# Sixteen weight requests on ScalarE's queue, a later check of alpha, and an early ScalarE copy in a gated-recurrence and SoLU kernel

## The chip, the cores and the metric

The kernel runs on one core of a Trainium2 chip. The metric is device microseconds of one execution. A run of the kernel before has seven such times; one more execution was taken by the hardware profiler, and all durations below are from that one.

## The reference

The computation is a gated linear recurrence over 768 tokens for 4 batches and 8 heads of width 48, and behind it a feed-forward block with a SoLU activation and a layer norm. Shapes and types that matter: q, k, v and alpha are float32 of (4, 8, 768, 48); w_in is (384, 1024) and w_out (1024, 384), both float64.

```python
for t in range(S):
    state = alpha[:, :, t, :, None] * state + np.einsum('bhd,bhe->bhde', k[:, :, t], v[:, :, t])
    y[:, :, t] = np.einsum('bhd,bhde->bhe', q[:, :, t], state)
...
h = x @ w_in                      # x is y as (tokens, 384)
h_max = np.max(h, axis=-1, keepdims=True)
e = np.exp(h - h_max)
sm = e / (np.sum(e, axis=-1, keepdims=True) + 1e-09)
solu = h * sm
mu = np.mean(solu, axis=-1, keepdims=True)
var = np.mean((solu - mu) ** 2, axis=-1, keepdims=True)
ln = (solu - mu) / np.sqrt(var + 1e-06) * g_ln
return (ln @ w_out).astype(np.float32)
```

## The kernel before

**Tiles and stages.** The 768 tokens are cut into six groups (g) of 128 tokens, each for all four batches. A group goes through the recurrence in matrix form (products of alpha by scans, masked scores, read-out y), and then through the feed-forward block: eight up-projections (f = 0 to 7, 512 token columns each) and the down-projections. Each head's 48 columns are split into 32 and 16; four heads' 32 rows fill the 128 partitions of one chunk, and the eight 16-row rests fill a third chunk.

**Order.** The order on every engine is written out by hand (a manual schedule): each engine takes its instructions in the order of the program text, and so does each DMA queue, SyncE's and ScalarE's. A DMA request is an instruction of the engine whose queue it goes on. A ScalarE request therefore takes ScalarE's time in its place in that order, and a wait of the request is a wait of all that stands behind it on ScalarE. Semaphores are placed by the framework; each request signals its landing on one of eight semaphores, which the requests of both queues take in turn.

**The start, group 0.** SyncE loads alpha (into `an`), k (`kn`), q (`qn`) and v, in this order; ScalarE requests four small constants (ident, mask, parity, g_rows). GpSimd clears buffers and later copies v into place (L180). TensorE runs `warm` (L422) and then turns alpha, k and q by matmuls with the identity (`turned`, L162). Ahead of each turning, ScalarE copies the last 16 columns of every head together (`ends_of`, L153), and the last third of the turning reads that copy. ScalarE copies turned alpha into `aT` (L655). VectorE scans it backwards (`scan_back`), multiplies k (L663), scans forward (`scan_on`, three parts) and multiplies q (L671): the last third first, giving `qe`, which ScalarE spreads by `apart` (L237). `alpha_over` (L201) is two ScalarE activations over the whole of `an`, whose accumulated sums a check at the end of the kernel reads. Then come the scores (L268), the mask products on VectorE (`masked`, L279), the read-out into four PSUM banks y (L300), ScalarE's four copies of y into `x` (L331), and `keys_back` (TensorE L287, ScalarE L289), whose transposes use three of the banks that y held.

**Weights.** w_in and w_out arrive as float64 words in six slots of a buffer, `room`. VectorE turns them into float32 with five instructions for a block of 768 columns (`bits`, L572 to L584); ScalarE tests their range with two activations, each with a read of its sum (`in_range`, L559 and L560). `fetch(i, slot, n)` requests block i; with n = 2 a double block (i and i + 1). For w_in a double block takes 16 requests: eight of 32 rows and eight of 16 rows, of 4 KB each row. `fetch(0, 3, 2)` and `fetch(2, 1, 2)` request all of w_in, 32 requests on SyncE behind v. `bits(0)` and `bits(1)` make the columns for f = 0 to 3 out of the first double block.

**The up stage of group 0** (the loop over f behind `in_range(1)`). `up_mm` is three matmuls (L366, which the profile shows as six), then `up_act`: Exp on ScalarE (L380), a product on VectorE (L381), Square on ScalarE (L382). PSUM has two banks for h, so that f + 2 waits for the product of f. In f = 0 follows `next_state` (TensorE L342, ScalarE L349), and the requests for w_out and the k, q and alpha of group 1.

```python
    masked(0)
    masked(1)
    bits(0)
    read_values(0)
    gains()
    keys_back(0)
    in_range(0)
    bits(1)
    in_range(1)
```

Of the kernel before, what the change touches and what calls it, by code (L numbers as in the profile page):

```python
# [11 lines left out]
U32 = mybir.dt.uint32  # L12
# [20 lines left out]
def fast_path(ctx, tc, q, k, v, alpha, moe_w_in, moe_w_out, moe_g_ln, out):  # L33
# [12 lines left out]
    nc = tc.nc  # L46
    B, H, S, D = q.shape
# [32 lines left out]
    ones = const.tile([P, P], FP, name="ones")  # L80
# [8 lines left out]
    mean_sb = const.tile([P, DM], FP, name="mean_sb")  # L89
# [10 lines left out]
    an = const.tile([P, H, TQ, D], FP, name="an")  # L100
# [36 lines left out]
    def by_token(x):  # L137

        return x.rearrange("p h u d -> p (h u d)").rearrange("p (b h d) -> p b h d", b=B, h=H)

    def load_first(src, dst, g):
        t = slice(g * P, (g + 1) * P)
        for b in range(0, B, 2):
            nc.sync.dma_start(
                out=by_token(dst)[:, b : b + 2].rearrange("p b h d -> p (b h) d"),
                in_=src[b : b + 2, :, t].rearrange("b h p d -> p (b h) d"),
            )

    def ends_of(src, tag=None):

        ends = ring.tile([P, T4], FP, name=tag) if tag else two.tile([P, T4], FP, tag="two", name="ends")
        ends = ends.rearrange("p (b d) -> p b d", b=B)
        nc.scalar.copy(out=ends.rearrange("p b (h d) -> p b h d", h=H), in_=by_token(src)[:, :, :, E0:D])  # L153
        return ends

    def turned(src, ends, out, blocks=range(NB)):

        x = by_token(src)
        for j in blocks:
            for b in range(B):  # L160
                cols = x[:, b, j, 0:E0] if j < H else ends[:, b, E0 * (j - H) : E0 * (j - H) + E0]
                nc.tensor.matmul(  # L162
                    out[j // NP][32 * b : 32 * b + 32, j % NP], lhsT=cols, rhs=ident, start=True, stop=True,
                    tile_position=(0, 32 * b), skip_group_check=True,
                )
# [9 lines left out]
    def load_v_first(slot):  # L175
        x = slots[slot].rearrange("p (n d) -> p n d", d=D)
        y = vn.rearrange("p b h d -> p (b h) d")
        nc.sync.dma_start(out=x, in_=v[:, :, 0:P].rearrange("b h p d -> p (b h) d"))
        for dst, src in ((slice(0, E0), slice(0, E0)), (slice(48, 64), slice(E0, D))):
            nc.gpsimd.tensor_copy(out=y[:, :, dst], in_=x[:, :, src])  # L180
# [16 lines left out]
    def alpha_over(g):  # L197
        x = an.rearrange("p h u d -> p (h u d)")
        sq = one.tile([P, 768], FP, name="sq").bitcast(U8)[:, 0 : x.shape[1]]
        for i, sign in enumerate((1.0, -1.0)):  # L200
            nc.scalar.activation(  # L201
                out=sq, in_=x, func=AF.Relu, scale=sign, bias=mone, accum_out=over[:, g, i : i + 1]
            )
# [12 lines left out]
    def scan_on(g, i):  # L216
        part = slice(NP * i, NP * i + NP)
        s = seed[i % 2]
        if i == 2:
            nc.vector.tensor_copy(out=fend[:, g], in_=h4[:, :, 1])  # L220

        least = small.tile([P, NP, 1], FP, name="least")
        nc.vector.tensor_scalar(out=least, in0=h4[:, part, 1:2], scalar1=LEAST, scalar2=None, op0=ALU.max)  # L223
        nc.vector.reciprocal(out=s[:, :, 0:1], in_=least)
        scan(aT[:, part], aT[:, part], s, False)
# [9 lines left out]
    def apart():  # L235
        for i in range(2):
            nc.scalar.mul(  # L237
                out=qv[:, H : 2 * H].rearrange("p (j i) t -> p j i t", i=2)[:, :, i], in_=qe, mul=parity[:, i : i + 1]
            )
# [16 lines left out]
    def quarter(b):  # L256
        return slice(32 * b, 32 * b + 32)

    def banks(name, shape, n=B):
        return [ps_a.tile([P] + shape, FP, tag=f"a{b}", name=f"{name}{b}") for b in range(n)]  # L260

    def scores(g, half, a=None):
        a = a or banks("a", [NP, P])
        for i in range(NP):
            h = half * NP + i
            for kb, qb in ((h, h), (H + h // 2, H + h)):
                for b in range(B):
                    nc.tensor.matmul(  # L268
                        a[b][:, i], lhsT=kT[quarter(b), kb], rhs=qv[quarter(b), qb], start=kb == h, stop=kb != h,
                        tile_position=(32 * b, 0), skip_group_check=True,  # L270
                    )
        masks[half] = a
# [21 lines left out]
    parts = [(a, [(NP * a + r, slice(0, E0)) for r in range(NP)]) for a in range(2)]  # L294
# [231 lines left out]

    raws = {}

    def fetch(i, slot, n=1):

        kind, f = pieces[i]
        w = n * F // (2 if kind else KC)
        raw = room[:, 1536 * slot : 1536 * (slot + n)].bitcast(U32).rearrange("p (c f w) -> p c f w", f=w, w=2)
        if kind:
            parts = [(slice(0, P), c, moe_w_out[(f + c) * P : (f + c + 1) * P, :]) for c in range(2)]
        else:
            rows = moe_w_in[:, f * P : f * P + w].rearrange("(h d) f -> h d f", d=D)
            parts = [(slice(E0 * r, E0 * r + E0), c, rows[NP * c + r, 0:E0]) for c in range(2) for r in range(NP)]
            parts += [(slice(E1 * h, E1 * h + E1), 2, rows[h, E0:D]) for h in range(H)]
        for rows, c, src in parts:  # L540
            if float64:
                nc.sync.dma_start(out=raw[rows, c].rearrange("p f w -> p (f w)"), in_=src.bitcast(U32))
            else:
                dst = w_out[rows, f + c, 0:DM] if kind else w_in[rows, c, f * P : f * P + w]
                nc.sync.dma_start(out=dst, in_=src)
        for m in range(n):
            raws[i + m] = raw[:, :, w // n * m : w // n * (m + 1)]

# [70 lines left out]
    def inline(x, name):  # L619
        return nc.inline_tensor(np.ascontiguousarray(x, np.float32), name=name).ap()  # L620

    load_first(alpha, an, 0)
    nc.scalar.dma_start(out=ident, in_=inline(np.eye(P), "ident_c"))
    nc.scalar.dma_start(out=mask, in_=inline(np.triu(np.ones((P, P))), "mask_c"))
    odd = np.arange(P) // E1 % 2
    nc.scalar.dma_start(out=parity, in_=inline(np.stack([1 - odd, odd], 1), "parity_c"))
# [9 lines left out]
        nc.gpsimd.memset(s, 0.0)  # L636
    nc.gpsimd.memset(state, 0.0)
    load_v_first(0)
    fetch(0, 3, 2)
    fetch(2, 1, 2)  # L640
    nc.vector.memset(ones, 1.0)
    nc.vector.memset(small_ones, 1.0 / 32)
    nc.vector.memset(mhalf, -0.5)
    nc.vector.memset(mone, -1.0)
# [2 lines left out]
    def three(name, where):  # L647
        return [pool.tile([P, NP, P], FP, tag=tag, name=f"{name}{i}") for i, (pool, tag) in enumerate(where)]
# [1 line left out]

    warm(18)
    t = three("tp_a", [(ps_a, "a0"), (ps_a, "a1"), (ps_a, "a2")])
    turned(an, ends_of(an), t)
    for i in range(3):
        nc.scalar.copy(out=aT[:, NP * i : NP * i + NP, 1:SW], in_=t[i])  # L655
        scan_back(0, i)
    t = three("tp_k", [(ps_a, "a3"), (ps_h, "h"), (ps_h, "h")])
    turned(kn, ends_of(kn), t)
    alpha_over(0)
    scan_on(0, 2)  # L660
    for i in range(3):
        part = slice(NP * i, NP * i + NP)
        nc.vector.tensor_tensor(out=kT[:, part], in0=t[i], in1=hk[:, part], op=ALU.mult)  # L663
    scan_on(0, 0)
    t = three("tp_q", [(ps_o, "o"), (ps_o, "o"), (ps_a, "a0")])
    turned(qn, ends_of(qn), t)
    for i in (2, 0, 1):
        if i == 1:
            scan_on(0, i)
        part = slice(NP * i, NP * i + NP)  # L670
        nc.vector.tensor_tensor(  # L671
            out=qe if i == 2 else qv[:, part], in0=t[i], in1=aT[:, part, 1:SW], op=ALU.mult
        )
        if i == 2:
            apart()
    scores(0, 0)
    t = [x.tile([P, NP, P], FP, tag=n, name="a_" + n) for x, n in ((ps_h, "h"), (ps_o, "o")) for _ in range(2)]
    scores(0, 1, t)
# [11 lines left out]
    for f in range(FC):  # L690
        p = 2 + f // 2
# [162 lines left out]
    for g in range(1, G + 1):  # L854
# [10 lines left out]
        for s in range(FC):  # L865
# [14 lines left out]
            if todo:  # L880
                n, half = todo.pop(0)
# [18 lines left out]
    parts = [N * 3, G * 2, G * NB] + [len(pieces)] * 2  # L900
    ends = np.cumsum([0] + parts)
# [4 lines left out]
    def compare(out, x, bound, op):  # L906
# [6 lines left out]
        out=chunks[:, :, 2], in0=sums[:, :, 2], scalar=0.25, in1=sums[:, :, 3], op0=ALU.mult, op1=ALU.is_le  # L913
# [6 lines left out]
    else:  # L920
# [9 lines left out]
        out=bad, in0=all_ok[0:1, 0:1], scalar1=float(P * ends[-1]), scalar2=None, op0=ALU.is_lt  # L930
# [415 lines left out]
def kernel(tc, *args):  # L1346

    with ExitStack() as ctx:
        taken = fast_path(ctx, tc, *args)
    with tc.If(taken > 0):  # L1350
        general_path(tc, *args)
# [30 lines left out]
```

## Time and profile before

| | |
|---|---|
| median of 7 runs | 399.08 us (396.38 to 401.43) |
| the profiled execution | 401.91 us |
| its span in the profile | 400.1 us |
| TensorE busy | 377.9 us, 94% |
| VectorE busy | 254.6 us, 64% |
| ScalarE busy | 146.2 us, 37% |
| GpSimd busy | 115.7 us, 29% |
| mean granted TensorE clock | 0.984 |

Times in the profile are counted from the start of the span. Engines are PE (TensorE's matmuls), PEld (its weight loads), DVE (VectorE), ACT (ScalarE), POOL (GpSimd) and SP (SyncE); an engine's name with a q is its sequencer, which issues DMA requests. L with a number is a line of the kernel before. The time of a DMA request is that of its issue; its landing comes later. Requests and waits of a sequencer are not counted as busy time.

### The profile page before, as it was taken

To read this page: it belongs to the slowest core of one execution; us is meant where nothing else is said; L and a number is where in the kernel's file an instruction comes from. 1 tells how busy PE (TensorE), PEld (TensorE's weight loads), DVE (VectorE), ACT (ScalarE), POOL (GpSimd) and SP (SyncE) were. 2 spreads that over 40 slices of the span, in tenths; PEclk is the share of its full clock that TensorE was granted. 3 is DMA by queue.
4 is the path that set the end of the run, shared out by engine and by line. 5 is a ranking of instruction groups with operands and counts; after the bars stand their busy time and mean duration, and the time that the engine had idled before them with its cause. 6 is when DMAs were issued, how large, how long until landed. Compare 5 with 4: busy or idle time off the path is not lost. (4 is left out here: it accounts for less than half of the span.)

```text
span 400.1 us, 11123 instructions
## 1 busy us (share of the span) xinstructions
PE 377.9 (94%) x4929; PEld 229.1 (57%) x4929; DVE 254.6 (64%) x415; ACT 146.2 (37%) x253; POOL 115.7 (29%) x118
## 2 busy tenths in 40 slices
PE   8786999977989999999999999999999999999995
PEld 8672435545674467556557555666556575555552
DVE  0968788997797868694574884664865413444510
ACT  2634575545314525225153243343152132223100
POOL 5010000022031893428130456210475110333200
PEclk9996999998999999999999999999999999999998
DMA  9966969601366302914040921004300000000011
GB/s 187 184 163 162 235 195 177 141 0 43 98 162 99 80 3 62 153 47 99 2 102 24 157 77 44 2 23 72 29 20 21 23 3 21 20 20 14 28 41 48
DMA packets 86409, 30.82 MB, mean 77 GB/s; under 512 B 67912, under 2 KB 84560, under 8 KB 86352
## 3 DMA queue, kind: packets, MB, share of 16 engines
q1 hardware_dynamic: 85328, 29.11, 33.9%
q8 instruction: 40, 0.66, 0.8%
q10 hardware_dynamic: 1024, 0.92, 0.7%
q14 instruction: 17, 0.14, 0.1%
HBM read 25.30 MB, written 4.72 MB: 75 GB/s over the span
## 5 line engine op out<-in xcount | busy, mean ns | idle before, releaser
L366 PE MATMUL h<-x,w_in 128*128 128x512 f32 x288 | 135.2, 610 | 4.4 <-DVE g_col L596 4.4
L477 PE MATMUL o<-w_out,room 128*128 128x385 f32 x384 | 133.2, 491 | 1.1 <-DVE least L223 1.1
L477 PEld LDWEIGHTS o<-w_out,room 128*128 128x128 f32 x384 | 71.4, 189 | 57.1 <-issue 15.5
L366 PEld LDWEIGHTS h<-x,w_in 128*128 128x128 f32 x288 | 53.3, 192 | 64.2 <-issue 51.2
L381 DVE TENSOR_TENSOR room<-h,e 128x512 f32<-128x512 f32 x40 | 27.8, 694 | 61.6 <-ACT e L380 61.6
L508 POOL TENSOR_TENSOR r<-sums,mhalf 128x1 f32<-128x1 f32 x20 | 12.2, 608 | 170.1 <-DVE sums L500 170.1
L380 ACT ACTIVATE e<-h 128x512 f32<-128x512 f32 x40 | 23.9, 596 | 91.7 <-PE h L366 91.7
L397 POOL TENSOR_TENSOR p<-p,e 128x512 f32<-128x512 f32 x30 | 41.0, 1367 | 24.7 <-ACT e L380 24.4
L382 ACT ACTIVATE u<-room 128x512 f32<-128x512 f32 x40 | 25.2, 631 | 42.4 <-DVE room L381 42.4
L279 DVE TENSOR_TENSOR sT<-a,mask 128x512 f32<-128x512 f32 x44 | 27.3, 682 | 16.0 <-PE a L268 16.0
L268 PE MATMUL a<-qv,kT 32*128 32x128 f32 x704 | 26.6, 291 | 4.9 <-DVE qv L758 2.0
L268 PEld LDWEIGHTS a<-qv,kT 32*128 32x128 f32 x704 | 23.6, 198 | 12.1 <-DVE qv L758 2.9
L397 DVE TENSOR_TENSOR p<-p,u 128x512 f32<-128x512 f32 x30 | 25.0, 833 | 8.6 <-ACT u L382 8.6
L209 DVE TENSOR_TENSOR_SCAN hT<-aT,unit 128x516 f32<-128x516 f32 x18 | 22.3, 1287 | 8.3 <-ACT aT L655 8.2
L209 DVE TENSOR_TENSOR_SCAN aT<-aT,seed 128x516 f32<-128x516 f32 x18 | 25.7, 1428 | 0.6
L300 PE MATMUL y<-sT,vn 128*32 128x128 f32 x768 | 22.8, 274 | 1.4 <-issue 0.8
L300 PEld LDWEIGHTS y<-sT,vn 128*32 128x32 f32 x768 | 20.7, 110 | 4.1 <-issue 2.6
L233 POOL TENSOR_TENSOR kT<-kT,hT 128x1024 f32<-128x1024 f32 (+1 forms) x8 | 13.3, 1686 | 30.9 <-DVE kT L184 30.9
L331 ACT COPY x<-y 128x384 f32<-128x384 f32 x24 | 11.2, 481 | 26.5 <-PE y L300 26.5
L300 PEld LDWEIGHTS y<-qv,state 32*32 32x32 f32 x1280 | 15.3, 103 | 7.6 <-issue 4.1
L300 PE MATMUL y<-qv,state 32*32 32x128 f32 x1280 | 19.0, 278 | 0.0
L201 ACT ACTIVATE sq<-an,mone 128x1536 uint8<-128x1536 f32 x12 | 18.8, 1571 | 0.2
(140 smaller groups left out, 372.5 us busy)
## 6 DMA issues: line engine op xcount, KB each, us to landing
an<-in_alpha_dram SPq DMA_DIRECT2D x20, 192.0 KB, 4.1
out_dram<-o_sb SPq DMA_DIRECT2D x20, 192.0 KB, 1.9
room<-in_moe_w_out_dram SPq DMA_DIRECT2D x8, 384.0 KB, 3.9
kn<-in_k_dram SPq DMA_DIRECT2D x16, 192.0 KB, 3.8
qn<-in_q_dram SPq DMA_DIRECT2D x16, 192.0 KB, 3.5
vn<-in_v_dram SPq DMA_DIRECT2D x5, 512.0 KB, 5.7
room<-in_moe_w_in_dram SPq DMA_DIRECT2D x16, 128.0 KB, 3.6
kn<-in_k_dram SPq DMA_DIRECT2D x4, 384.0 KB, 5.7
```

The costliest lines, as they stand in the source:

```text
L201: nc.scalar.activation(out=sq, in_=x, func=AF.Relu, scale=sign, bias=mone, accum_out=over[:, g, i : i + 1])
L209: nc.vector.tensor_tensor_scan(out=o, data0=a, data1=s, initial=1.0, op0=ALU.mult, op1=ALU.add)
L233: nc.gpsimd.tensor_tensor(out=kT[:, part], in0=kT[:, part], in1=hk[:, part], op=ALU.mult)
L268: nc.tensor.matmul(a[b][:, i], lhsT=kT[quarter(b), kb], rhs=qv[quarter(b), qb], start=kb == h, stop=kb != h, tile_position=(32 * b, 0), sk ...
L279: nc.vector.tensor_tensor(out=sT[:, b, half * NP : half * NP + NP], in0=a[b], in1=mask[:, None, :].to_broadcast([P, NP, P]), op=ALU.mult,)
L300: nc.tensor.matmul(y_bank(b)[quarter(r), a], lhsT=lhsT, rhs=rhs, start=(b, r) not in begun, stop=stop, tile_position=(row, 32 * r), skip_g ...
L366: nc.tensor.matmul(h, lhsT=w_in[:, a, f * P : (f + 1) * P], rhs=d["x"][:, a].rearrange("p b t -> p (b t)"), start=(a == 0), stop=(a == KC ...
L380: nc.scalar.activation(out=e, in_=h, func=AF.Exp)
L381: nc.vector.tensor_tensor(out=u, in0=h, in1=e, op=ALU.mult)
L382: nc.scalar.activation(out=u2, in_=u, func=AF.Square)
L397: eng.tensor_tensor(out=p, in0=d[0][i] if f == 1 else p, in1=d[f][i], op=ALU.add)
L477: nc.tensor.matmul(d["o"][:, 0 : DM + 1], lhsT=u_of(g, f)[:, b * P : b * P + P], rhs=w_out[:, f], start=(f == 0), stop=(f == FC - 1), skip ...
```

## The change

`fetch` takes a queue and a slice of its requests. The first two double blocks of w_in are requested in two halves: the eight 32-row requests of each stay on SyncE's queue in their old place, and the eight 16-row requests of each go on ScalarE's queue. There, five of the first block stand ahead of the `ends_of` copy of q (the copy is now issued inside the call of `turned` as before), three behind it, and the eight of the second block behind `apart`. `alpha_over(0)` moves from behind the turning of k to behind these requests. For the turning of alpha the copy of the ends is written as a statement of its own. A ScalarE copy of one column, from `ones` into `mean_sb`, which is written anew before it is read, is put between the requests for ident and mask, and the memset of `ones` is moved ahead of it.

```diff
-    def fetch(i, slot, n=1):
+    def fetch(i, slot, n=1, queue=nc.sync, some=slice(None)):
...
-        for rows, c, src in parts:
+        for rows, c, src in parts[some]:
             if float64:
-                nc.sync.dma_start(out=raw[rows, c].rearrange("p f w -> p (f w)"), in_=src.bitcast(U32))
+                queue.dma_start(out=raw[rows, c].rearrange("p f w -> p (f w)"), in_=src.bitcast(U32))
...
     load_first(alpha, an, 0)
     nc.scalar.dma_start(out=ident, in_=inline(np.eye(P), "ident_c"))
+    nc.vector.memset(ones, 1.0)
+    nc.scalar.copy(out=mean_sb[:, 0:1], in_=ones[:, 0:1])
     nc.scalar.dma_start(out=mask, in_=inline(np.triu(np.ones((P, P))), "mask_c"))
...
     load_v_first(0)
-    fetch(0, 3, 2)
-    fetch(2, 1, 2)
-    nc.vector.memset(ones, 1.0)
+    fetch(0, 3, 2, some=slice(0, H))
+    fetch(2, 1, 2, some=slice(0, H))
...
-    turned(an, ends_of(an), t)
+    ends = ends_of(an)
+    turned(an, ends, t)
...
     turned(kn, ends_of(kn), t)
-    alpha_over(0)
     scan_on(0, 2)
...
     t = three("tp_q", [(ps_o, "o"), (ps_o, "o"), (ps_a, "a0")])
+    fetch(0, 3, 2, nc.scalar, slice(H, H + 5))
     turned(qn, ends_of(qn), t)
+    fetch(0, 3, 2, nc.scalar, slice(H + 5, 2 * H))
...
         if i == 2:
             apart()
+    fetch(2, 1, 2, nc.scalar, slice(H, 2 * H))
+    alpha_over(0)
     scores(0, 0)
```

More of the change, by code (lines that the diff above doesn't have):

```diff
@@ L539, in fetch @@
             parts += [(slice(E1 * h, E1 * h + E1), 2, rows[h, E0:D]) for h in range(H)]
-        for rows, c, src in parts:
+        for rows, c, src in parts[some]:
             if float64:
-                nc.sync.dma_start(out=raw[rows, c].rearrange("p f w -> p (f w)"), in_=src.bitcast(U32))
+                queue.dma_start(out=raw[rows, c].rearrange("p f w -> p (f w)"), in_=src.bitcast(U32))
             else:
                 dst = w_out[rows, f + c, 0:DM] if kind else w_in[rows, c, f * P : f * P + w]
-                nc.sync.dma_start(out=dst, in_=src)
+                queue.dma_start(out=dst, in_=src)
         for m in range(n):
```

## The prediction

> **What bounds the kernel now.** I began with the page's slices and its chain of waits. The chain is of no use: it ends in the last output copies at 0%. The slices (10 us each) show where TensorE falters.
>
> ```profile
> PE   8786999977989999999999999999999999999995
>
> ```
>
> TensorE is busy 377.9 of 400.1 us, nearly gapless from slice 10 on; slice 3 (30 to 40 us) has both its thinnest work and its lowest clock. So time gained before 40 us can last to the end, and time lost there too. Next, the waits of the first 60 us (waiter, releaser: us in total, times, longest):
>
> ```profile
> PE h L366 <- DVE g_col L596: 4.4, 1, 4.4
> DVE top L572 <- DMA room<-in_moe_w_in_dram: 3.0, 1, 3.0
> ACT x L331 <- PE y L300: 6.7, 4, 5.6
> ```
>
> The first up-projection waits for VectorE's conversion of w_in (bits), and that waited for the transfer of the first double block. Its place, in the timeline (start, length, engine, line; in brackets the idle time before and its releaser):
>
> ```profile
> 13.08 21.60 SPq L542 DMA_DIRECT2D room<-in_moe_w_in_dram  x32
> 11.08 1.58 ACT L201 ACTIVATE sq<-an,mone 128x1536 uint8<-128x1536 f32 x1
> 14.73 0.62 ACT L153 COPY ends<-qn 128x512 f32<-128x512 f32 x1 [0.28 <-DMA qn<-in_q_dram]
> 18.54 1.33 ACT L237 ACTIVATE qv<-qe,parity 128x512 f32<-128x512 f32 x2 [3.20 <-DVE qe L671]
> 25.43 0.48 ACT L331 COPY x<-y 128x384 f32<-128x384 f32 x1 [5.55 <-PE y L300]
> 24.96 1.28 DVE L279 TENSOR_TENSOR sT<-a_o,mask 128x512 f32<-128x512 f32 x2
> 29.28 0.95 DVE L572 TENSOR_SCALAR top<-room 128x768 uint32<-128x768 uint32 x1 [3.04 <-DMA room<-in_moe_w_in_dram]
> 33.96 5.43 PE L366 MATMUL h<-x,w_in 128*128 128x512 f32 x6 [4.36 <-DVE g_col L596]
> ```
>
> SyncE issues 32 requests one by one; the sixteenth, which completes the first double block, is issued at 25.56 and lands at 29.10 (from the trace's semaphore events). VectorE was free at 26.24. ScalarE has holes of 3.2 us and 5.6 us in the same stretch. Last, the stretches by window (busy us of PE, PEld, DVE, ACT, POOL, then clock, DMA share, GB/s):
>
> ```profile
> 23.00:29.00 6.00, 5.43 (x161) 4.82 (x155) 3.24 (x6) 2.16 (x5) 0.00 (x0) 1.00 0.43 111
> 29.60:33.96 4.36, 0.00 (x1) 0.04 (x1) 4.22 (x7) 4.26 (x9) 0.00 (x0) 0.82 0.87 225
> 33.96:39.30 5.34, 5.34 (x6) 1.81 (x6) 4.21 (x5) 0.23 (x2) 0.00 (x0) 0.51 0.37 91
> ```
>
> From 23 to 29 us the DMA engines are busy 43%: issue, not bandwidth, holds the block back. And after the idle 4.36 us the clock is at half: the six matmuls take 5.43 us, against 0.43 us apiece (2.6) from 41.22 on.
>
> **What the Trainium skill says.** "DMA: Bandwidth & Descriptors", section "Issuing engines are not separate DMA queues", says that a second issuing engine saves only the sequencer's time; the 43% agrees that this is what is short here. The same page, "Anatomy of one DMA", says that a wait for a semaphore happens on the issuing sequencer before dispatch. The trace agrees: requests take eight semaphores in turn, shared by both queues (the ident request on ScalarE and the first q request on SyncE use one), and the sixteenth w_in request started at 25.56, just after the one eight before it had landed at 25.38. "TensorE: Matmul & The Clock Gate", section "Part 1: The HAM clock gate", says that an idle window of about 3.4 us halves the clock until a busy one; the trace has 0.5 from 32.41 to 39.23, two such windows.
>
> **The change, part by part** (times on the clock of the profile before).
>
> *Early copy.* The table load, 1.28 us at 6.77 behind alpha's landing, moves to about 1.0, beside the warm-up matmuls. The first aT copy then waits for tp_a alone (its 16 pairs are done near 8.05): the scans start near 8.8, not 9.27, 0.5 us less on VectorE. The requests for mask, parity and g_rows, behind the load, go out some 1.5 us later; their readers come at 18.5 or after: nothing. The memset of ones was VectorE's first anyway: nothing.
>
> *SyncE.* Sixteen of 32 requests leave its queue; pitch there is 0.46 us (0.42 and a gap). The first block keeps eight, the last issued at 20.67 before. I allow 22.6, as each waits for the semaphore of one eight before it in the mixed order, and 25.5 for the landing.
>
> *ScalarE, requests.* Sixteen issues. ScalarE's four at the start took 0.39 to 0.67, so 0.46 each, 7.4 us in all. Five sit ahead of the ends copy of qn: 11.0 to 13.3, in the hole that alpha_over leaves, before q has landed (14.65): hidden. Their 320 KB fall beside q's tail; I give that 0.4 us on q, so tp_q ends near 17.9 and VectorE's 0.5 us gain is used up: VectorE is free near 26.5. Without cover five issues would cost 2.3 us on q's path. Three issues after that copy fit before apart (18.54). Eight follow apart, from 20.3 (19.87 plus the shift). With two queues alternating over eight semaphores each queue has four in flight; 64 KB requests landed 3.1 us after issue (median). So four go at once (b1 not before v, landed 20.28 before, say 21.2), and the other four go as the first land: 23.4 to 25.8. Bounds: 24.0 without such waits, 29 if each waits for a late landing; I take 25.8.
>
> *alpha_over.* It goes from a free place at 11.08 to 14.46 into a full one: two times 1.57 and 0.19 is 3.5 us, 25.8 to 29.3. Behind it on ScalarE stand the four x copies (4 x 0.48): 29.3 to 31.2, not 25.43 to 28.53. Its reader, the check near the end, is far.
>
> *Who waits.* VectorE: bits(0) from 26.5, 4.52 us, ends 31.1, not 33.80; bits(1) at 35.6, not 38.39. TensorE: keys_back needs the banks that the x copies free, so it ends near 31.3; up_mm(0,0) starts at 31.4, not 33.96. Its window now holds the transposes and the matmuls, so it runs at full clock, 2.6 us: done at 34.0, not 39.3. ScalarE now bounds: kg copies to 32.8, in_range(0) and (1) 4.0 us to 36.8 (34.19 before), Exp 36.85, not 39.43. From here the order of before: product (VectorE) 37.5 to 38.2, Square to 38.9, two state copies (1.06) to 39.9, Exp of f=1 to 40.5 (TensorE had h at 38.6), product to 41.3, Square to 42.0, in_range(2) 1.9 to 43.9, Exp of f=2 to 44.5, product to 45.2. That product frees the bank for f=4: TensorE starts it at 45.25, not 49.23.
>
> The sum: the up stage is ahead by 4.0 us at f=4. The second half of w_in (at most 32 us) and the k, q and w_out loads that start from conversions 2 to 3 us earlier stay ahead of their readers. Nothing later has a fixed time, so the 4.0 lasts: 400.1 to 396.1 in the span. The profiled execution took 401.91 us, 1.8 around the span; the median shown is 2.8 below that, 399.08. I take 4.0 off it: **395.1**.
>
> **Rivals.**
>
> *No stall on ScalarE* (each request at 0.46): alpha_over ends at 27.5, in_range at 34.9, VectorE's bits(1) at 35.6 decides, f=4 starts near 43.7: 5.5 us, 393.6. For it: latency is 2.3 us for some requests. Against: at most four in flight.
>
> *Given back on ScalarE.* The last requests go at 29 instead of 25.8, waiting for landings on the other queue; everything behind slips by 3.2, leaving 0.8: 398.3. In this group also: TensorE idle long enough to halve the clock again, or DMA contention that delays v's landing and with it y. For it: v's and q's last share landed 1 to 1.7 us after the rest, so landings straggle. Against: DMA share 0.43 leaves room.
>
> *Slower: the five requests hold the ends copy of qn.* SyncE's own first w_in request took 4.76 us (13.08 to 17.84) behind v's. If ScalarE's five likewise wait, [...] for landings of w_in requests (the first landed at 20.87), the fifth goes out at 23, the ends copy slips from 14.73 to 23, tp_q and the qe product by 7.6, and apart, the eight requests, alpha_over and x behind: Exp near 44.5, f=4 near 52.9, 3.7 us late: 402.8. It decides from an ends copy later than about 21.5: up to there the slack of ScalarE and the regained clock pay. For it: program text puts those five after sixteen SyncE requests, and only the time order of issue, which I read from the semaphores of the first eight requests (an's second half numbered after g_rows), keeps them clear of it. Against: that same order, and ScalarE's issues at 1.6 to 2.8 us, 0.45 and 0.67 long beside a SyncE issue of 1.44.
>
> *The change does nothing* would need w_in not to be the release; the 3.0 us wait excludes it.
>
> **How the numbers follow.** Main case 0.42 (own range 392.5 to 397), no stall 0.14, given back 0.19 (397 to 401), slower 0.25. A difference under 0.5% (2 us) can hardly be told from none here. So faster is 0.42 + 0.14 + 0.02, same 0.17, slower 0.25. The range takes in all but the worst of the slow case and the quickest: 391.5 to 402.
>
> **What would show it.** Right: bits(0) starts within 1 us of VectorE's last mask product; the clock stays at 1.0 through 32 to 39; ScalarE has no wait in front of the ends copy of qn; x copies start at 28 to 30; f=4 near 45. Wrong: the ends copy of qn after 18, a hole on ScalarE of over 6 us among its requests, or x copies after 32.

## The result

The kernel after takes 403.08 us (median of 26 runs, 401.05 to 404.24), the kernel before, in runs beside it, 398.68 us (63 runs, 396.38 to 402.91). The ratio is 1.010, 95% interval 1.008 to 1.012: slower by 1%. The prediction was 395.1, with 402 as its upper end and a chance of 0.25 for slower.

The profiled execution of after took 402.0 us with a span of 400.1 us, the same span as that of before. One plain fact is needed to read that: the times of the kernel before lie in groups, 26 of the 63 at 396.4 to 397.8 us, 14 near 399 and 23 at 400.4 to 402.9, and its profiled execution (401.91) was one of the upper group. After has only one group. So the two profiles agree in span where the medians differ by 4.4 us; what parts the upper group from the rest is TensorE's clock, shown in the experiments below.

The slices of after, 10 us each: TensorE's busy share and its granted clock; the last row is the granted clock of before.

```profile
PE   8685999977979999999999999999999999999995
...
PEclk9996999999999999999999999999999999999998
...
PEclk9996999998999999999999999999999999999998
```

The dip in slice 3 (30 to 40 us) is not filled; the clock there is again 0.6. Next, what the engines waited for in after's first 60 us (waiter, releaser: us in total, times, longest).

```profile
ACT sq L201 <- DMA room<-in_moe_w_in_dram: 9.2, 1, 9.2
...
PE tp L287 <- ACT x L331: 4.8, 1, 4.8
```

VectorE's wait for the first double block shrank from 3.0 to 1.7 us, but only because VectorE came later (free at 27.66 us, 26.24 in before). In its place stand a 9.2 us hole of ScalarE ahead of `alpha_over`, among its own requests, and a 4.8 us hole of TensorE that waits for ScalarE's x copies. The places, in after's timeline (start, length, engine, line; idle time before in brackets):

```profile
16.41 0.62 ACT L153 COPY ends<-qn 128x512 f32<-128x512 f32 x1 [5.29 <-DMA qn<-in_q_dram]
...
22.71 7.78 ACTq L542 DMA_DIRECT2D room<-in_moe_w_in_dram  x8
30.54 1.58 ACT L201 ACTIVATE sq<-an,mone 128x1536 uint8<-128x1536 f32 x1 [9.24 <-DMA room<-in_moe_w_in_dram]
...
33.81 1.60 ACT L331 COPY x<-y 128x384 f32<-128x384 f32 x4
...
29.40 0.95 DVE L572 TENSOR_SCALAR top<-room 128x768 uint32<-128x768 uint32 x1 [1.74 <-DMA room<-in_moe_w_in_dram]
...
34.33 2.82 PE L287 MATMUL tp<-ident,kT 128*128 128x128 f32 x12 [4.77 <-ACT x L331]
36.94 3.82 PE L366 MATMUL h<-x,w_in 128*128 128x512 f32 x6
```

The eight requests of the second block take 7.8 us from first to last, `alpha_over` follows, then the x copies at 33.81 (25.43 in before), and with them everything of TensorE. `bits(0)` starts at 29.40, against 29.28: the first double block is not a moment earlier. The windows of after (us; busy us of PE, PEld, DVE, ACT, POOL with their instructions; clock, DMA share, GB/s):

```profile
23.00:29.00 6.00, 5.43 (x184) 5.04 (x188) 4.66 (x8) 0.00 (x0) 0.62 (x3) 1.00 0.78 202
29.60:36.94 7.34, 2.61 (x12) 2.62 (x13) 7.03 (x10) 6.02 (x10) 0.00 (x0) 0.68 0.71 144
```

From 23 to 29 us ScalarE computes nothing at all, while the DMA engines are busy 78% instead of 43%: the first block's 32-row requests, which before had gone ahead of its 16-row ones, come last now, and the second block's stand between them. From 29.6 to 36.94 TensorE works 2.6 of 7.3 us, and its clock falls again, at 32.3 us.

**Why the requests waited.** From the semaphore events of after's trace, with the landing of the request that had the same semaphore before:

```
request (issue start)                 the semaphore came free
SyncE, block 1, third        21.93    21.91  v landed
SyncE, block 1, fourth       22.29    17.10  early ScalarE request landed; queued behind the third
ScalarE, block 2, first      22.71    22.69  block 1, SyncE's first
ScalarE, block 2, second     23.07    23.00  block 1, SyncE's second
ScalarE, block 2, third      24.55    24.53  block 1, SyncE's third
ScalarE, block 2, fourth     26.78    26.76  block 1, SyncE's fourth
ScalarE, block 2, last       30.18    30.15  block 2, ScalarE's fourth
```

Eight semaphores serve both queues, so at most eight requests are in flight, whichever engine issues them, and each waits for the one eight places earlier in one common order. A request takes the semaphore whose turn it is, not one that is free: SyncE's third stood from 19.08 to 21.93 us for v's, while two of the eight, those of the early ScalarE requests, had been free since 17.10 and 17.41. A request took 2.2 to 5.7 us to land here. The 26 requests of after that were issued from 16.43 to 32.51 us came 0.64 us apart (16.08 / 25); in before, the 31 from 17.88 to 34.26 came 0.55 us apart (16.38 / 30). Two queues issued no faster than one. The early requests also changed the order: in before, the request that reuses v's semaphore is the first block's eighth, issued at 20.67 with v landed at 20.28, so that it didn't wait; in after it is SyncE's third, and it stood until v landed at 21.91.

The section "Issuing engines are not separate DMA queues" of the Trainium skill's "DMA: Bandwidth & Descriptors" says that a second issuing engine saves only the sequencer's time to start a transfer. Here it saved not even that.

### The profile page after: what moved, and what is told of

Same layout as the page of the kernel before. It is cut to its first block, busy times and chain, and to the rows that moved or that the text cites. A ratio compares the mean times of both kernels' runs of the same rounds, so it can differ in the third digit from the quotient of the medians.

```text
span 400.1 us, 11120 instructions
## 1 busy us (share of the span) xinstructions
PE 375.6 (94%) x4929; PEld 228.3 (57%) x4929; DVE 254.5 (64%) x415; ACT 146.3 (37%) x254; POOL 115.5 (29%) x118
## 3 DMA queue, kind: packets, MB, share of 16 engines
q1 hardware_dynamic: 84816, 28.06, 33.9%
## 5 line engine op out<-in xcount | busy, mean ns | idle before, releaser
L366 PE MATMUL h<-x,w_in 128*128 128x512 f32 x288 | 133.4, 603 | 0.0
L268 PE MATMUL a<-qv,kT 32*128 32x128 f32 x704 | 25.0, 278 | 4.5 <-DVE qv L763 2.0
L268 PEld LDWEIGHTS a<-qv,kT 32*128 32x128 f32 x704 | 22.0, 186 | 11.7 <-DVE qv L763 2.9
L300 PEld LDWEIGHTS y<-sT,vn 128*32 128x32 f32 x768 | 20.7, 110 | 4.4 <-issue 2.9
```

What stands on the lines that cost most here:

```text
L268: nc.tensor.matmul(a[b][:, i], lhsT=kT[quarter(b), kb], rhs=qv[quarter(b), qb], start=kb == h, stop=kb != h, tile_position=(32 * b, 0), sk ...
L300: nc.tensor.matmul(y_bank(b)[quarter(r), a], lhsT=lhsT, rhs=rhs, start=(b, r) not in begun, stop=stop, tile_position=(row, 32 * r), skip_g ...
L366: nc.tensor.matmul(h, lhsT=w_in[:, a, f * P : (f + 1) * P], rhs=d["x"][:, a].rearrange("p b t -> p (b t)"), start=(a == 0), stop=(a == KC ...
```

## The experiments

The letters in the expectations: A, the second block's requests (and what stands behind them) hold ScalarE; B, the early ScalarE requests make q late; C, the check of alpha in its new place is all the loss; D, eight requests in flight are the limit, whichever queue they are on. Key points of every profiled execution, in us of its span; "halved" is where the clock record shows 0.5 before 100 us:

| kernel | time, median | bits(0) | first x copy | f = 0 | f = 4 | halved |
|---|---|---|---|---|---|---|
| before (profile 401.91) | 398.68 | 29.28 | 25.43 | 33.96 | 49.23 | 32.4-39.2, 93.8-97.3 |
| before, a second profile (396.74) | | 27.93 | 27.08 | 32.60 | 45.26 | 20.0-23.5 |
| after | 403.08 | 29.40 | 33.81 | 36.94 | 50.61 | 32.3-39.1 |
| second block back on SyncE | 398.61 | 28.49 | 26.85 | 33.16 | 45.92 | none |
| alpha check back | 400.58 | 31.01 | 32.95 | 35.66 | 48.43 | 22.7-26.1, 94.4-97.8 |
| alpha check alone | 399.73 | 29.24 | 25.48 | 33.91 | 49.46 | 33.0-39.9, 94.5-97.9 |
| early copy alone | 399.15 | 28.83 | 25.87 | 33.50 | 47.85 | 33.9-37.3 |
| before, bridged | 397.75 | 28.34 | 25.42 | 33.01 | 45.66 | 90.9-94.4 |
| after, bridged | 403.41 | 30.55 | 34.14 | 36.02 | 49.05 | 93.9-97.3 |
| four and four | 401.35 | 29.52 | 25.26 | 34.19 | 49.45 | 32.6-39.4, 94.0-97.5 |
| v behind sixteen | 402.16 | 26.40 | 31.32 | 37.11 | 49.85 | 28.0-34.8 |
| v behind sixteen, bridged | 403.58 | 26.40 | 32.31 | 38.82 | 51.42 | 28.6-35.4, 96.9-100.3 |
| v behind four | 399.01 | 28.37 | 25.45 | 33.04 | 47.25 | 32.8-36.2 |
| v behind eight | 397.64 | 27.88 | 27.15 | 32.54 | 45.19 | 20.7-24.2 |

Where a ratio is given below, it is to the kernel before in runs beside it.

### The second block's requests back on SyncE

After, with one part undone:

```diff
-    fetch(2, 1, 2, some=slice(0, H))
+    fetch(2, 1, 2)
...
-    fetch(2, 1, 2, nc.scalar, slice(H, 2 * H))
     alpha_over(0)
```

> The eight 16-row requests of the second double block go back on SyncE's queue; all else as in the changed kernel. Theory A (ScalarE is held by those eight requests, which wait for landings between 22.7 and 30.5 us, with alpha_over and the x copies behind): ScalarE is free after apart (21.3), alpha_over ends by 25, the x copies follow TensorE's y (first near 26.9), the first up-projection starts near 32 at full clock and f=1 near 38.5, against 42.60 in the changed kernel and 41.22 before: 4 us less than the changed kernel, 2 to 3 us less than before. Theory B (the five early requests make q and v late, and with them VectorE): the gain stays away, f=1 starts at 41 or later and the time is that of the changed kernel within 1.5 us.

Measured: 398.61 us (22 runs, 397.60 to 400.97), ratio 0.998 (0.9955 to 1.0008). That is 4.5 us below after, 1% of it, and all of the loss. Its timeline:

```profile
21.20 1.56 ACT L201 ACTIVATE sq<-an,mone 128x1536 uint8<-128x1536 f32 x1
...
26.85 0.48 ACT L331 COPY x<-y 128x384 f32<-128x384 f32 x1 [2.28 <-PE y L300]
...
33.16 2.81 PE L366 MATMUL h<-x,w_in 128*128 128x512 f32 x6 [2.15 <-DVE g_col L596]
```

`alpha_over` now runs at once behind `apart`, in a hole, and ends 2.3 us before the first x copy is wanted. The x copies wait for TensorE, not for ScalarE. f = 0 starts 3.8 us earlier than in after, and its clock is whole (2.81 us against 3.82). At f = 4 the lead is 4.7 us, close to the 4.5 of the medians. So the eight requests of the second block, with the check of alpha queued behind them, are the loss, as theory A has it. The 2 to 3 us under before that were expected too did not come: with the eight requests away, the rest of the change gains nothing that can be told from zero. VectorE was free at 27.66, 1.4 us later than in before, and the first block landed at 28.31. Even with its clock whole this execution is at f = 4 no earlier than before's second profile (45.92 against 45.26).

### The check of alpha in its old place, the requests as in after

This kernel has also no early copy.

```diff
-    nc.vector.memset(ones, 1.0)
-    nc.scalar.copy(out=mean_sb[:, 0:1], in_=ones[:, 0:1])
...
     turned(kn, ends_of(kn), t)
+    alpha_over(0)
     scan_on(0, 2)
...
     fetch(2, 1, 2, nc.scalar, slice(H, 2 * H))
-    alpha_over(0)
     scores(0, 0)
```

> Requests as in the changed kernel, alpha_over back behind the turning of k, no early copy. Theory A: the eight requests still end near 30, but the x copies start there and not at 33.8: the up stage starts 3 us earlier than in the changed kernel; f=1 near 39.5, bounded by the conversion of the first block (29.4 plus 4.5): 3 us less than the changed kernel. Theory C (alpha_over's 3.5 us in the full place is all the loss): the same number, with the requests costing nothing: the wait in front of the x copies would be gone. Theory B: 1 us or less is gained, since q and v stay late.

Measured: 400.58 us (22 runs, 399.67 to 402.11), ratio 1.0045 (1.0018 to 1.0071): 2.5 us better than after, still slower than before. Its timeline:

```profile
17.88 4.13 ACTq L542 DMA_DIRECT2D room<-in_moe_w_in_dram  x3
22.06 1.33 ACT L237 ACTIVATE qv<-qe,parity 128x512 f32<-128x512 f32 x2 [4.42 <-DVE aT L209]
24.74 8.17 ACTq L542 DMA_DIRECT2D room<-in_moe_w_in_dram  x8
32.95 1.25 ACT L331 COPY x<-y 128x384 f32<-128x384 f32 x3 [9.56 <-PE y L300]
```

The first line shows the fear of the slower rival, in a milder form: behind `alpha_over` the requests come later, the ends copy of q starts at 17.02 (14.73 in before) behind the fifth of them, the three behind that copy no longer find a free semaphore (the second and third go at 21.22 and 21.62, just after landings at 21.20 and 21.60), and `apart` stands until 22.06 (18.54 in before). The releasers named in the brackets (`aT`, y) had long been done when ScalarE went on; what held it was the requests ahead in its own order. The eight then take 8.2 us and the x copies start at 32.95, not near 30 as expected, so that 2.5 of the expected 3 us came back. The wait in front of the x copies that C would have gone is still there. So the requests alone make the kernel slower, and with the check behind them (and the early copy) it is 2.2 us more at f = 4 (48.43 against 50.61).

### The two small parts, each alone

To the kernel before, the check of alpha moved behind `apart`:

```diff
-    alpha_over(0)
     scan_on(0, 2)
...
             apart()
+    alpha_over(0)
     scores(0, 0)
```

> The kernel before, with alpha_over alone moved behind apart. ScalarE is idle there for 5.55 us (19.87 to 25.43), so 3.5 us fit: theories A and B expect the time of before within 0.3% and the first x copy near 25.4. Theory C expects it late, by 3 us in the x copies, and a slower kernel only if the first block's conversion (33.8) is not later anyway: still the time of before.

Measured: 399.73 us (22 runs), ratio 1.0004 (0.997 to 1.004). The first x copy starts at 25.48 (25.43 in before), and not 3 us later as C has it. The place behind `apart` is as free as the old one, as long as no requests stand in it.

And the early copy alone:

```diff
     nc.scalar.dma_start(out=ident, in_=inline(np.eye(P), "ident_c"))
+    nc.vector.memset(ones, 1.0)
+    nc.scalar.copy(out=mean_sb[:, 0:1], in_=ones[:, 0:1])
     nc.scalar.dma_start(out=mask, in_=inline(np.triu(np.ones((P, P))), "mask_c"))
...
-    nc.vector.memset(ones, 1.0)
```

> The kernel before with the early ScalarE copy alone. The table load is hidden and the scans start 0.3 us earlier (8.96 in the changed kernel, 9.27 before); VectorE then waits for the first block of w_in as before. All theories expect the time of before within 0.3%.

Measured: 399.15 us (12 runs), ratio 1.001 (0.997 to 1.006): nothing. In its profile the scans didn't even start earlier (9.72, 8.96 expected): the turning of alpha started only at 7.88 there, behind `warm` (7.18 in before). And what the copy may give VectorE is hidden by the wait for the first block.

### Only the first block's requests on ScalarE, none ahead of q

The first block's eight 16-row requests go on ScalarE, four behind the ends copy of q and four behind `apart`; the second block is whole on SyncE and the check of alpha in its old place (the early copy stays). Against after:

```diff
-    fetch(2, 1, 2, some=slice(0, H))
+    fetch(2, 1, 2)
...
     turned(kn, ends_of(kn), t)
+    alpha_over(0)
...
-    fetch(0, 3, 2, nc.scalar, slice(H, H + 5))
     turned(qn, ends_of(qn), t)
-    fetch(0, 3, 2, nc.scalar, slice(H + 5, 2 * H))
+    fetch(0, 3, 2, nc.scalar, slice(H, H + 4))
...
-    fetch(2, 1, 2, nc.scalar, slice(H, 2 * H))
-    alpha_over(0)
+    fetch(0, 3, 2, nc.scalar, slice(H + 4, 2 * H))
```

> Only the first double block's eight 16-row requests go on ScalarE, four behind the copy of q's ends and four behind apart; the second block is all on SyncE, alpha_over back behind the turning of k, early copy kept. No request stands ahead of q's ends copy, and q has landed before they go. If early requests made q late (theory B), q lands by 14.8 and VectorE is free by 26.3; if the eight shared semaphores set the pace (theory D: eight in flight, each 3 to 4.5 us until it lands, whichever queue issues), the first block still lands no earlier than 27 us and the time is near that of the kernel with the second block back on SyncE, 398.6 us; if SyncE's issue time set it, the block lands by 25.5 and the time is 396.5 or less.

Measured: 401.35 us (22 runs, 396.51 to 402.77), ratio 1.003 (0.999 to 1.006). The time is a miss; what was expected of q and of the block came. Its timeline:

```profile
14.73 0.62 ACT L153 COPY ends<-qn 128x512 f32<-128x512 f32 x1 [0.19 <-DMA qn<-in_q_dram]
14.75 1.75 ACTq L542 DMA_DIRECT2D room<-in_moe_w_in_dram  x4
...
21.64 2.09 ACTq L542 DMA_DIRECT2D room<-in_moe_w_in_dram  x4
25.26 0.48 ACT L331 COPY x<-y 128x384 f32<-128x384 f32 x1 [5.55 <-DMA room<-in_moe_w_in_dram]
...
29.52 0.95 DVE L572 TENSOR_SCALAR top<-room 128x768 uint32<-128x768 uint32 x1 [3.44 <-DMA room<-in_moe_w_in_dram]
...
34.19 5.41 PE L366 MATMUL h<-x,w_in 128*128 128x512 f32 x6 [4.76 <-DVE g_col L596]
```

With no requests ahead of q, q landed at 14.65, as in before, against 16.33 in after and in the kernel with the second block back: B is right about q, though q is not the loss. VectorE was free at 26.07. Each queue had eight of the block's requests, ScalarE lost nothing that counted, and the block still landed at 29.34 (29.10 in before). From 18.43 to 21.64 us nothing was issued on either queue: all eight semaphores were taken, v's among them, and the next two requests went 0.02 us after landings (21.64 after 21.62, 21.81 after v's 21.79). That is what D expects: a second queue brings the block no earlier. The last lines tell where the time went: VectorE then waited 3.4 us, TensorE 4.8 us, and the clock was at half for f = 0, in this execution and probably in 14 of the 22: so many lie above 400 us, with a mean granted clock of 0.984 to 0.989 (five lie below 397.5, where before's lower group is). The number of semaphores itself wasn't varied, so D rests on the matched times of issue and landing and on this run.

### TensorE's clock: the kernel before once more, and both kernels bridged

The kernel before itself was profiled again, to see what parts its groups.

> The kernel before itself, profiled once more. Its times lie in two groups, near 397 and near 401.5. If the half-clock stretch at 93.8 us is what parts them, a run near 397 has no such stretch and is otherwise the same to within 0.3 us until 90 us; if the start parts them, f=1 does not start at 41.2.

It took 396.74 us, an execution of the lower group. Its row of the granted clock:

```profile
PEclk9989999999999999999999999999999999999998
```

The half clock lies at 20.0 to 23.5 us, on the scores, and not in the first up-projection. The scores in this profile, then in the first one:

```profile
19.61 3.46 PE L268 MATMUL a<-qv,kT 32*128 32x128 f32 x64 [2.08 <-DVE least L223]
...
19.25 2.08 PE L268 MATMUL a<-qv,kT 32*128 32x128 f32 x64 [1.74 <-DVE least L223]
```

The slow scores put off what follows: the first x copy starts at 27.08 instead of 25.43, and VectorE is free at 27.88 instead of 26.24. But the first block landed at 27.75 there, so hardly any of this delay counts. In the first up-projection a half clock counts in full: f = 0 took 2.8 us and f = 1 started at 37.24 here, against 5.4 us and 41.22 in the first profile. At f = 4 this execution is 4.0 us ahead, at the end of its span 5.2. Of that, 1.4 us stand before f = 0 and are not clock (the block landed at 27.75 and not at 29.10), 2.6 arise from f = 0 to f = 4, and the rest behind, where the first profile has a second half clock.

The mean granted clock of every execution says the same. In the 163 times of the kernel before that were taken beside the experiments, all 61 above 400 us have 0.984 to 0.989, and all 71 up to 397.8 have 0.992 to 0.998. The middle group has 0.990 to 0.996, so what parts it from the lower one stays open. Open too is what decides where the half clock falls: TensorE stood idle for 4.36 us ahead of f = 0 in the first profile and for 1.35 in the second, and the request behind v's load was held for 4.8 us in one and 3.3 in the other.

Then matmuls were added whose result isn't used, to keep TensorE busy: eight in the kernel before, behind `keys_back(0)`, where it waits for `bits(0)`; sixteen in after, ahead of `keys_back(0)`, where it waits for the x copies. (The profile shows each of them as two.)

```diff
     keys_back(0)
+    warm(8)
     in_range(0)
```

> The kernel before, with eight extra 128x128 matmuls (some 1.7 us) on TensorE between keys_back(0) and the first up-projection; their result is not used. If the two groups of its times (near 397 and near 401) come from the halved TensorE clock in the first up-projection, the clock stays at 1.0 from 30 to 40 us, the group near 401 disappears and the median falls to 397 or lower, 0.5% under before. If they come from the transfers, both groups stay.

Measured: 397.75 us (22 runs, 396.86 to 399.09), ratio 0.9989 (0.9966 to 1.0012). No time lies above 399.1, where beside it 16 of 51 of the kernel before lay above 400. The timeline:

```profile
29.42 1.95 PE L422 MATMUL warm<-ones 128*128 128x128 f32 x16
33.01 2.81 PE L366 MATMUL h<-x,w_in 128*128 128x512 f32 x6 [1.63 <-DVE g_col L596]
```

The upper group needs the half clock in the first up-projection: with TensorE kept busy there it is gone. The median gains less than expected (0.1%, not to be told from zero); this profile still has one half-clock stretch, from 90.9 us on.

```diff
+    warm(16)
     keys_back(0)
```

> The changed kernel, with sixteen extra 128x128 matmuls (some 3.4 us) on TensorE ahead of keys_back(0), in the 4.8 us in which it waits for the x copies; their result is not used. If the loss is ScalarE's lateness plus the clock that the idle time halves, the first up-projection still starts at 36.9 but takes 2.6 and not 3.8 us, and f=1 follows the Exp of ScalarE (41.5) rather than TensorE: 1 to 1.5 us less than the changed kernel, still 0.5% slower than before. If the clock is no part of it: no change.

Measured: 403.41 us (6 runs, 402.44 to 405.23), ratio 1.013 (1.007 to 1.019). A miss: 1 to 1.5 us less than after was expected. The timeline:

```profile
36.02 2.74 PE L366 MATMUL h<-x,w_in 128*128 128x512 f32 x6
...
41.03 0.58 ACT L380 ACTIVATE sT<-h 128x512 f32<-128x512 f32 x1
```

The clock held and f = 0 took 2.7 us in place of 3.8, but the Exp behind it starts at 41.03, only 0.5 us earlier than in after (41.53): ScalarE is still busy with the range tests that its own delay pushed back. So the clock is a follower in after, not the cause; ScalarE is. This execution was 1.6 us ahead of after at f = 4 and ended later: its last matmul starts at 395.64, after's at 394.76. It has a half clock from 93.9 us on that after's profile doesn't have, and by 99 us the lead was gone. The six times don't say more.

### Does the place in the order matter, if the queue doesn't?

If D holds, the first block comes earlier only by standing earlier in the one order. The kernel before, with v's load behind the block:

```diff
-    load_v_first(0)
     fetch(0, 3, 2)
+    load_v_first(0)
     fetch(2, 1, 2)
```

> The kernel before, with one move: the loads of v are requested behind the sixteen requests of w_in's first double block instead of ahead of them, all still on SyncE's queue. Theory D (at most eight requests are in flight, so the first block comes earlier only if it stands earlier in the one order, not if it is issued by a second engine): the block's sixteen requests go from about 10 to 17 us and land by 20 to 23 us, against 29.1; bits(0) then starts when VectorE is free, at 26 to 27 instead of 29.3; v lands near 23 to 24, y follows, the x copies end near 29.5 and the first up-projection starts at 31 to 32. Time 395 to 397 us, ratio 0.99 to 0.995, if TensorE's clock stays whole there. Rival V (v is as urgent as the block): v lands after 25, the x copies start after 28 and the first up-projection starts no earlier than 33.5: ratio 0.998 to 1.005.

Measured: 402.16 us (14 runs, 401.27 to 403.44), ratio 1.008 (1.005 to 1.012). Its timeline:

```profile
26.40 0.94 DVE L572 TENSOR_SCALAR top<-room 128x768 uint32<-128x768 uint32 x1
...
29.28 6.38 PE L300 MATMUL y<-sT,vn 128*32 128x128 f32 x128 [5.46 <-POOL vn L180]
...
31.32 0.48 ACT L331 COPY x<-y 128x384 f32<-128x384 f32 x1 [11.20 <-PE y L300]
```

The first half of D's expectation came true on SyncE alone: the block landed at 23.08, and VectorE went from its last mask product into `bits(0)` without a wait, at 26.40. The second half failed, and rival V took its place: v, issued at 20.68, landed at 28.11, and y, x and `keys_back` waited for it. The time lies above what V had expected as well. TensorE's clock is part of that: TensorE stood for 5.5 us ahead of the read-out, the clock was at half from 28.0 to 34.8, and the read-out took 6.4 us (3.9 in before). The same with four idle matmuls behind `keys_back(0)`:

> The same move of v's loads, and four matmuls more behind keys_back(0), whose result is not used: they only keep TensorE busy ahead of the first up-projection. Theory D with the clock theory: like the run without them, but the clock is whole from 31 to 39 us in every execution: 394 to 396.5 us, ratio 0.988 to 0.993, and the spread of the times under 3 us. Rival V: the first up-projection starts no earlier than 33.5, ratio 0.996 to 1.000 from the clock alone.

Measured: 403.58 us (6 runs), ratio 1.013 (1.007 to 1.019), above both expectations: V again; TensorE had been idle for v before that place, so the matmuls do not save the clock (half from 28.6 to 35.4) and only stand ahead of f = 0, which started at 38.82.

Between the two ends lies v behind some of the sixteen (`fetch` with a slice, first `slice(0, 4)` or `slice(0, 8)`, then v, then the rest), with four idle matmuls behind `keys_back(0)` in both; the expectation of the first says eight, the kernel had four.

> The kernel before, with v's loads requested behind four of the sixteen requests of w_in's first double block, and eight matmuls more behind keys_back(0), whose result is not used and which only keep TensorE busy there. Theory D with v as urgent as the block: v lands near 22 to 23 (20.3 in the kernel before, 28.1 behind all sixteen), the block near 28 (29.1 and 22.3); x copies from 25.5 to 27, bits(0) from 28, first up-projection near 32.3 at a whole clock: 396 to 398 us, ratio 0.994 to 0.998. If the slow landing of v (7.4 us behind all sixteen) comes back with only four ahead, v lands after 25 and the ratio is 1.00 or more.

> As the run before it, with v's loads behind eight of the sixteen requests, and four matmuls more in place of eight. Theory D: v lands near 24.5, the block near 27; x copies from 27 to 28, bits(0) from 27 to 27.5, first up-projection near 32: 396 to 398.5 us, ratio 0.994 to 1.000. If v then lands after 26, x decides and the ratio is above 1.002.

Measured: 399.01 us (22 runs), ratio 1.002 (0.999 to 1.005), and 397.64 us (14 runs), ratio 0.9987 (0.995 to 1.002). Behind four, v landed at 22.10 and the block at 28.19, both as expected, and f = 0 started at 33.04, but at half clock (32.8 to 36.2 us), which the expectation did not have; the time is a miss. Behind eight, v landed at 24.00 and the block at 27.54, and the timeline shows the balance:

```profile
27.15 0.48 ACT L331 COPY x<-y 128x384 f32<-128x384 f32 x1 [6.58 <-PE y L300]
27.88 0.94 DVE L572 TENSOR_SCALAR top<-room 128x768 uint32<-128x768 uint32 x1
```

f = 0 starts at 32.54, like the good execution of before. Within what was measured neither beats the kernel before: what the block gains v loses.

## Why the prediction was wrong

**What was right.** The early copy was put at 0.5 us for VectorE: the scans start at 8.96 instead of 9.27, 0.3 us (within what executions differ by: before's second profile has 9.64). The five requests ahead of the ends copy of q did not hold ScalarE: they went out from 10.40 to 12.82, and the copy waited for q's landing alone. The place of failure was foreseen as a rival, "given back on ScalarE", and among what would show the prediction wrong stood a hole of over 6 us among ScalarE's requests and x copies after 32. Both came: 9.2 us, and 33.81.

**First failed step: SyncE's half of the block.** "I allow 22.6 ... and 25.5 for the landing." Its last request went at 25.02 and landed at 29.09. That issue time was short in before was read rightly: none of its 32 requests waited for a semaphore, each started 0.04 to 0.05 us behind the end of the one ahead. That holds for the sixteenth too, which the prediction took for a case of the wait: its semaphore had been free for 0.18 us. But 0.18 us is hardly any room, and the change used it up. SyncE's first request stood until 18.61 behind v's load, as in before (17.84); its third, which now had the turn of v's semaphore, stood for 2.8 us, until 21.93. The landing of the last then took 4.1 us and not the 2.9 allowed, with the second block's requests between (3.5 in the kernel without them on ScalarE). The rule was in the prediction's own text (the sixteenth request goes just after the one eight before it has landed), but it was used as a small correction, and the turn that v's semaphore takes in the new order was not worked out.

**Second: the eight requests.** "Four go at once ... and the other four go as the first land: 23.4 to 25.8", with 29 as the bound. They were issued from 22.71 to 30.18: the first 2.4 us later than the 20.3 assumed, and then 1.07 us apart (7.47 / 7). Five of the eight went 0.02 to 0.07 us after the landing that freed their semaphore. The wait for a landing, which the prediction kept for its far bound of 29, was the rule. So the last is 4.4 us late, `alpha_over` ends at 33.9 and not 29.3, and the Exp of f = 0 starts at 41.53 and not 36.85, 4.7 us late.

**Third: q.** "I give that 0.4 us on q." It was 1.7 (16.33 against 14.65), and VectorE was free at 27.66, not 26.5. With the block landing at 29.1 this cost nothing more.

**Fourth: the clock.** "Its window now holds the transposes and the matmuls, so it runs at full clock." TensorE instead stood for 4.8 us ahead of the transposes, and the clock was half from 32.3: 1.2 us more for f = 0 (3.82 against 2.6). By the run with the clock bridged, only 0.5 us of that reached the Exp of f = 0. And the gain was counted from a profile of the upper group. In the lower group's profile the clock was whole there already: f = 0 took 2.8 us and f = 1 started at 37.24, so the 2.8 us of regained clock was not there to be had in those executions. "Part 1: The HAM clock gate" of the Trainium skill's "TensorE: Matmul & The Clock Gate" says that the window of activity runs freely and isn't tied to the kernel's start; the runs agree so far as the same program had its half clock at 32.4 in one execution and at 20.0 in another.

**The sum.** 403.08 - 395.1 is 8.0 us. The profiled execution of after took 402.0, where 396.1 + 1.8 = 397.9 was predicted: 4.1. Of that, f = 4 is 5.4 us late (50.61 against 45.25), and the half clock near 94 us, which before's profile had and after's lacks, gave 1.05 of it back by the start of the second group's up stage, and another 0.3 went by 143 us, for a reason that isn't shown. The other 3.9 is the step from a profile to a median: before's profile lies 2.8 above its median, after's 1.1 below its own. Taking 4.0 us off the median was wrong for that reason alone by some 3 us.

**The rivals.** "Given back on ScalarE" was the mechanism; its price, 398.3, kept the first block's early landing and the whole clock (the halved clock was named beside it, without a price), and the kernel had neither. The slower rival named 402.8, near the time measured, but that is luck: its ends copy was to be held by the five requests, and wasn't. "No stall on ScalarE" is excluded by the 9.2 us.

**What stays open.** Whether more than eight requests in flight would have brought the block earlier, or the DMA engines would then have been the limit: in after they were busy 85% from 16.43 to 32.51 us and moved 174 GB/s, in before 72% and 182 GB/s from 17.88 to 34.26. The number of semaphores wasn't tried.

## What to carry to other kernels

Before moving requests to a second queue, work out what limits them: requests in flight divided by their time to land gives a rate, and if all queues draw on the same semaphores, a second queue doesn't raise it; it only changes whose turn it is. If the turns are fixed, also find the request that gets the semaphore of a slow load: it waits even while others are free. A request on a compute engine's queue is an instruction of that engine: price it at a wait for a landing, not at its issue time, and count all that is queued behind it, above all what another engine's next step needs. And when the times of one kernel lie in groups, find out to which group the profile belongs before a stage's time is taken off the median.

## What the runs showed of the hardware

- 320 KB in five requests of 4 KB rows, issued on the second queue while q's second load was under way, made that load land 1.7 us later (16.33 against 14.65; 14.65 again with no requests ahead of it). v's load landed 1.5 to 1.6 us later with them and with four requests behind q alike (21.91 and 21.79, against 20.28).
- A load of v takes long to land wherever it stands: 10.3 us in before, 7.4 us behind sixteen requests of w_in (20.68 to 28.11), 6.7 behind eight; and the next request on its queue takes 3.0 to 5.7 us to issue, in place of 0.42, though its semaphore is free (in before from 13.08 to 17.84, free since 5.08).
- A request was said above to take ScalarE's time in its place in the order. While the instruction ahead still runs it doesn't: in the kernel with the alpha check back four were issued from 13.03 to 15.07 us beside `alpha_over`, whose second activation ran from 13.03 to 14.60. What a request costs ScalarE is its wait, borne by all that stands behind it: 9.2 us ahead of `alpha_over` in after.
- One kernel without any change had executions 4 to 5 us apart, mostly by where the half clock fell: 396.74 us with it at 20.0 to 23.5, where the delay was hidden behind a transfer, 401.91 us with it at 32.4 to 39.2 and 93.8 to 97.3. Eight idle matmuls (1.95 us) removed the upper group.
